# Routed experts behind attention and an MLP: two token tiles at a time, h made transposed, rows gathered an expert ahead

## The chip, the cores and the metric

The kernel runs on one core of a Trainium2 chip. The metric is the device time of one execution in microseconds (us); the median of three runs is given. A profile is one further execution, recorded by the hardware profiler.

## The reference

Three parts follow one another. Only the third is touched by most of the change.

1. Attention with a window of 128 over 4 batches, 8 heads, 576 positions, head size 64.
2. An MLP on the 2304 tokens of 512 features: `g = s * relu(x @ w_in)**2 + b`, `g @ w_out`, with 2048 hidden features.
3. Routed experts. A token is worked on if `x @ w_skip > 0`, else it passes unchanged. Its expert is the argmax of eight gate values:

```python
for e in range(E):                       # 8 experts, w1 512x1024, w2 1024x512
    mask = e_idx == e
    h = np.maximum(xc[mask] @ w1[e], 0.0)
    y[mask] = gate_w[mask, None] * (h @ w2[e])
out[do_compute] = xc + y
```

The reference, worked on its own drawn inputs, sends 639, 194, 63, 83, 51, 20, 167 and 143 tokens to the experts: 5, 2, 1, 1, 1, 1, 2 and 2 tiles of 128, 15 in all.

## The kernel before, in words

**Number format.** All big products use fp32r operands. Each fp32 operand is taken apart in a high part (a ScalarE cast) and a low part (VectorE, operand less high part), and a product is three matmuls: high x high, high x low, low x high.

**MLP.** `body` runs six blocks of 384 tokens; in a block, 16 slices of the hidden features (loop over `m`), each with 12 matmuls of 384 columns (`g1`) and 9 of 512 (`g2`). After a block its tokens are routed (`route`): logits, argmax, place in the list of the expert; three indirect DMAs on GpSimd (L625) write the list entries of the block, token number and gate weight, to DRAM (`lst`). In the last block the queue of SyncE (SP) also brings the first expert weights: `pump` (L637) issues a load of 512 KB for every free raw buffer, `split` (L644) makes the high and low part of one piece and frees its buffer. There are 8 pieces an expert: 0 to 3 are w1, 4 to 7 are w2. Five raw buffers (`ring`) serve the last block, one piece per `m`, and so all 16 pieces of experts 0 and 1; seven more (`more`) are added behind it. The parts of an expert lie in `eh` and `el` in one of two sets by the expert's parity.

**Routed experts.** `moe2` (L756) is a generator: `body` resumes it at certain points, so that the first tile of expert 0, made up of tokens of the first five blocks, is already worked on while the last block is routed. Entries of the last block that belong to tiles 1 and 2 of expert 0 are found by matmuls (`new`, L612), and their rows are gathered without waiting for the list in DRAM.

A tile goes through these steps. Its 128 rows come by an indirect DMA on GpSimd (`gather`, L780). TensorE turns them in four transposes (`x_t`, L786), ScalarE and VectorE make `xth` and `xtl`. `gemm1` (L795) has the tile's x as the loaded operand and w1 as the moving one: 24 matmuls of 512 columns, whose result, tokens by hidden features, ScalarE passes through relu (L799). `h_t` (L819) turns it in eight transposes into two banks; ScalarE and VectorE make `hth` and `htl` (L822, L823). `gemm2` (L805) is 24 matmuls of 512 columns. `fin` (L810) multiplies by the gate weight and adds the row, and an indirect DMA writes the rows out (L813).

**Order.** One `step` (L834) works on three tiles at once: it gathers tile n+1, does `gemm1` of tile n, then `gemm2` of tile n-1 with the turn of tile n+1's x between its halves, and last `h_t` of tile n. Rows and list entries are shifted from buffer to buffer by VectorE copies at the start of a step (`shift`, L826 and L827), ahead of the gather. ScalarE, VectorE and GpSimd take the order of the program here (`manual_schedule`). The splits of a step stand between its other work; `ahead` limits them to 4 pieces past the expert in work, 12 from its start.

**Branches.** The number of tiles of an expert is known only on the chip. `chain` (L882) has a branch per tile, up to `KMAX`, then a loop; `leave` (L871) is the step that goes over to the next expert. A `hint` after `gemm1` tells TensorE's instruction fetch which way the next branch goes.

Of the kernel before, what the change touches and what calls it, by code (L numbers as in the profile page):

```python
# [21 lines left out]
TB = 384  # L22
# [4 lines left out]
KMAX = (6,) + (2,) * 7  # L27
AHEAD = (0, 0, 1, 1, 1, 0, 0, 0)
BIG = 1 << 20
LE = 128 * 32  # L30
RING, MORE = 5, 7
UB = 3
CONV = (6, 7, 8, 9, 10, 11, 12)


def body(tc, q_in, k_in, vl, wm, we, wg, wgt, s_in, b_in, mask_in, cst_in, rout_in, ids_in, out):
# [488 lines left out]
    def route(j):  # L525
# [111 lines left out]
    def pump(eng=nc.sync):  # L637
        while ws.free and ws.loaded < 8 * NE:
            t, i = divmod(ws.loaded, 8)
# [4 lines left out]
    def split(t, i):  # L644
        n = 8 * t + i
# [38 lines left out]
    for j in range(NB):  # L684
# [15 lines left out]
        for m in range(NM):  # L700
# [26 lines left out]
            if j == NB - 1:  # L727
                split(*divmod(m, 8))
# [9 lines left out]
class Stream:  # L738


    def __init__(self):
        self.loaded, self.split, self.places, self.free, self.at = 0, 0, RING, [], {}

    def state(self):
        return self.loaded, self.split, self.places, list(self.free), dict(self.at)

    def back_to(self, st):
        self.loaded, self.split, self.places, self.free, self.at = *st[:3], list(st[3]), dict(st[4])
# [7 lines left out]
def moe2(tc, L):  # L756
# [4 lines left out]
    xg = [C.tile([128, DM], F32, name=f"xg{i}") for i in range(3)]  # L761
    lt = [C.tile([128, 2], U32, name=f"lt{i}") for i in range(3)]
    ls = [C.tile([128, 2], U32, name=f"ls{i}") for i in range(4)]
    la = C.tile([128, NE, NTILE, 2], U32, name="la")
    og = C.tile([128, DM], F32, name="og")
    xth = C.tile([128, DM], F32R, name="xth")
    xtl = C.tile([128, DM], F32R, name="xtl")
# [4 lines left out]
    extra = []  # L772
    bank = lambda tag, name, bufs=1: psum.tile([128, 512], F32, name=name, tag=tag, bufs=bufs)

    def gather(e, k, rows=NT, a=0):
        listed = e or not isinstance(k, int) or k not in (1, 2)
        if listed:
            nc.vector.tensor_copy(lt[a], la[:, e, k, :])
        idx = la[:, e, k, 0:1] if isinstance(k, int) and listed else lt[a][:, 0:1]
        nc.gpsimd.indirect_dma_start(  # L780
            out=xg[a], out_offset=None, in_=x2d[0:rows], in_offset=bass.IndirectOffsetOnAxis(ap=idx, axis=0),
            bounds_check=rows - 1, oob_is_err=False)

    def x_t(a=0):
        for k in range(4):
            last = nc.tensor.transpose(p_x[:, k * 128:(k + 1) * 128], xg[a][:, k * 128:(k + 1) * 128], ident)  # L786
        nc.scalar.copy(xth, p_x)
        nc.vector.tensor_tensor(out=xtl, in0=p_x, in1=xth.bitcast(F32), op=ALU.subtract)
        return last

    def gemm1(p, f, ks=range(4)):
        n = 3 * ks[0]
        todo = [(k, x, w[p, k]) for k in ks for x, w in ((xth, eh), (xth, el))] + [(k, xtl, eh[p, k]) for k in ks]
        for k, x, w in todo:
            nc.tensor.matmul(p_h[f], lhsT=x[:, k * 128:(k + 1) * 128], rhs=w[:, f * 512:(f + 1) * 512],  # L795
                             start=n == 0, stop=n == 11)
# [4 lines left out]
    def gemm2(p, f, cs=None):  # L801
# [7 lines left out]
    def fin(n):  # L809
        nc.vector.scalar_tensor_tensor(out=og, in0=p_o, scalar=lt[2][:, 1:2].bitcast(F32), in1=xg[2],  # L810
                                       op0=ALU.mult, op1=ALU.add)
# [12 lines left out]

    def shift(a):
        nc.vector.tensor_copy(lt[a + 1], lt[a])  # L826
        nc.vector.tensor_copy(xg[a + 1], xg[a])  # L827

    def hint(e, k):

        if e < NE and k < NTILE:
            tc.mark_branch_hint_location(f"tile{e}_{k}", hint=K[e] > k, engines=[mybir.EngineType.PE])

    def step(at, e1, e2, ahead, n=0, wider=0, then=None):  # L834
# [3 lines left out]
        pieces = list(range(ws.split, min(ahead, 8 * NE)))  # L838
        if e2 is not None:
            shift(1)  # L840
            shift(0)
        if at is not None and at not in ((0, 1), (0, 2)):
            gather(*at)

        def more(n):
            for _ in range(min(n, len(pieces))):
                split(*divmod(pieces.pop(0), 8))
        more(2)
        if e1 is not None:
            gemm1(e1 % 2, 0)  # L850
            more(2)
            gemm1(e1 % 2, 1)
            if then:
                hint(*then)
            for _ in range(min(wider, RING + MORE - ws.places)):
# [179 lines left out]
```

## Time and profile before

| | |
|---|---|
| Runs, median (lowest to highest) | 761.05 us (760.36 to 761.53) |
| Profiled execution | 759.11 us |
| its span | 757.0 us |
| TensorE (PE) busy | 731.1 us, 97% of the span |
| VectorE (DVE) busy | 532.4 us, 70% |
| ScalarE (ACT) busy | 384.4 us, 51% |
| GpSimd (POOL) busy | 53.7 us, 7% |

The span is the time between the first and the last instruction of the profile; the execution's own time is somewhat longer. PEld is the weight load that goes before a matmul; it may overlap PE. A busy TensorE is not TensorE at its peak, since a matmul is counted from its start to its modelled end: the spacing of starts tells what one costs. The routed experts' full steps run from about 568 us to the end.

### The profile page before, as it was taken

What the parts mean: (1) busy time and instruction counts of PE and PEld (TensorE: products, weight loads), DVE (VectorE), ACT (ScalarE), POOL (GpSimd) and SP (SyncE); (2) the same over time, 40 slices, a digit from 0 to 9 for tenths busy, and PEclk for the clock granted to TensorE, in tenths of its full rate; (3) what the DMA queues carried; (4) which work ended last, traced back from release to release, by engine and by line L of the source; (5) the groups of instructions that cost most, each with busy time, mean ns of one, the idle gap of its engine ahead of it and who ended that gap; (6) DMA issues with size and microseconds to landing.
All of it is one profiled execution on the core that took longest, in us unless ns stands there. A gap on an engine that the chain in (4) does not pass through costs nothing. (4 is left out here: it accounts for less than half of the span.)

```text
span 757.0 us, 12740 instructions
## 1 busy us (share of the span) xinstructions
PE 731.1 (97%) x4328; PEld 611.4 (81%) x4328; DVE 532.4 (70%) x1618; ACT 384.4 (51%) x909; POOL 53.7 (7%) x58
## 2 busy tenths in 40 slices
PE   7889999999999999999999999999999999899996
PEld 4568888888888888888888888989887878677884
DVE  4989999666686676777676665899642343999551
ACT  6767777544454445555564332545432243777440
POOL 0000000000001000100001000100211211112111
PEclk9689999999999999999999999999999999999999
DMA  8976341522313112422222111765443451898000
GB/s 248 304 261 195 117 124 50 164 77 73 92 47 132 53 57 67 147 71 74 57 88 95 43 42 29 271 174 167 126 153 106 137 189 44 287 349 324 18 23 16
DMA packets 50591, 96.38 MB, mean 127 GB/s; under 512 B 8554, under 2 KB 25962, under 8 KB 50496
## 3 DMA queue, kind: packets, MB, share of 16 engines
q1 hardware_dynamic: 45600, 85.82, 35.8%
q0 software_dynamic: 2976, 5.59, 2.3%
q10 hardware_dynamic: 1920, 3.80, 1.7%
q8 instruction: 47, 0.77, 0.4%
q14 instruction: 48, 0.39, 0.2%
HBM read 83.83 MB, written 13.65 MB: 129 GB/s over the span
## 5 line engine op out<-in xcount | busy, mean ns | idle before, releaser
L128 PE MATMUL h_ps<-xh,wh 128*128 128x384 f32 x380 | 132.5, 349 | 0.0
L128 PE MATMUL h_ps<-xh,wl 128*128 128x384 f32 x380 | 128.8, 339 | 0.4 <-DVE wl L70 0.4
L128 PE MATMUL h_ps<-xl,wh 128*128 128x384 f32 x380 | 128.6, 338 | 0.0
L460 ACT ACTIVATE r<-h_ps 128x384 f32<-128x384 f32 x96 | 47.1, 490 | 132.0 <-PE h_ps L128 111.9
L461 DVE SCALAR_TENSOR_TENSOR r<-r,sb 128x384 f32<-128x384 f32 x96 | 59.2, 616 | 64.0 <-ACT r L460 59.2
L522 DVE CUSTOM_DVE_ANT_0 junk<-x,hp 128x512 bf16<-128x512 f32 x135 | 92.8, 687 | 1.6
L171 ACT ACTIVATE tp<-tp,stat 128x256 f32<-128x256 f32 (+2 forms) x160 | 74.8, 469 | 28.0 <-DVE stat L163 27.9
L128 PE MATMUL acc<-wh,gh 128*128 128x512 f32 x288 | 86.8, 409 | 0.5 <-ACT gh L470 0.5
L128 PE MATMUL acc<-wh,gl 128*128 128x512 f32 x288 | 83.0, 397 | 0.0
L128 PE MATMUL acc<-wl,gh 128*128 128x512 f32 x288 | 82.4, 394 | 0.0
L471 DVE SCALAR_TENSOR_TENSOR gl<-r,sb,gh 128x384 fp32r<-128x384 f32 x96 | 59.0, 615 | 29.6 <-ACT gh L470 28.0
L470 ACT ACTIVATE gh<-r,sb 128x384 fp32r<-128x384 f32 x96 | 59.2, 616 | 40.5 <-DVE r L461 38.2
L128 PEld LDWEIGHTS h_ps<-xh,wh 128*128 128x128 f32 x380 | 71.8, 189 | 4.7 <-issue 1.4
L128 PEld LDWEIGHTS h_ps<-xl,wh 128*128 128x128 f32 x380 | 71.9, 189 | 2.4
L128 PEld LDWEIGHTS h_ps<-xh,wl 128*128 128x128 f32 x380 | 71.8, 189 | 0.7 <-DVE wl L70 0.7
L128 PEld LDWEIGHTS acc<-wh,gl 128*128 128x128 f32 x288 | 54.1, 189 | 13.2 <-DVE gl L471 0.4
L128 PEld LDWEIGHTS acc<-wl,gh 128*128 128x128 f32 x288 | 54.1, 188 | 12.6
L163 DVE CUSTOM_DVE_ANT_0 tp<-s_ps,masks 128x256 f32<-128x256 f32 (+2 forms) x160 | 52.9, 377 | 9.2 <-PE t_ps L126 4.0
L128 PEld LDWEIGHTS acc<-wh,gh 128*128 128x128 f32 x288 | 49.8, 188 | 7.9 <-issue 1.4
L625 POOL DMA_INDIRECT lst<-pay,di x18 | 18.8, 1047 | 470.7 <-DVE di L623 466.8
L805 PE MATMUL p_o<-wh,hth 128*128 128x512 f32 x120 | 48.9, 407 | 0.4 <-ACT hth L822 0.4
L795 PE MATMUL p_h<-wh,xth 128*128 128x512 f32 x120 | 48.8, 407 | 0.5 <-ACT hth L822 0.4
(138 smaller groups left out, 1245.0 us busy)
## 6 DMA issues: line engine op xcount, KB each, us to landing
ring<-we SPq DMA_DIRECT2D x36, 512.0 KB
w_words<-wm SPq DMA_DIRECT2D x30, 512.0 KB
hp<-wgt SPq DMA_DIRECT2D x45, 256.0 KB
more<-we SPq DMA_DIRECT2D x21, 512.0 KB
vt<-vl SPq DMA_DIRECT2D x32, 192.0 KB
x2d<-x SPq DMA_DIRECT2D x17, 256.0 KB
out<-x SPq DMA_DIRECT2D x17, 256.0 KB
more<-we ACTq DMA_DIRECT2D x7, 512.0 KB
```

The lines of the kernel that those rows point to most:

```text
L128: i = f(*args, **kw)
L163: anchor['v'] = nc.vector.tensor_tensor_reduce(out=t[0:nr, i, c0:c0 + n], in0=ps[i][0:nr, c0:c0 + n], in1=masks[0:nr, 2 * units[u][1] + i, ...
L171: anchor['s'] = nc.scalar.activation(out=t[0:nr, i, c0:c0 + n], in_=t[0:nr, i, c0:c0 + n], func=ACTF.Exp, scale=-1.0, bias=st[0:nr, 0, i:i ...
L460: nc.scalar.activation(out=r, in_=hp, func=ACTF.Relu)
L461: nc.vector.scalar_tensor_tensor(out=r, in0=r, scalar=sb[:, 0:1], in1=r, op0=ALU.mult, op1=ALU.mult)
L470: nc.scalar.activation(out=gh, in_=r, func=ACTF.Identity, bias=sb[:, 1:2])
L471: i = nc.vector.scalar_tensor_tensor(out=gl, in0=r, scalar=sb[:, 1:2], in1=gh.bitcast(F32), op0=ALU.add, op1=ALU.subtract)
L522: nc.vector.tensor_tensor_reduce(out=junk, in0=x2t[j, t], in1=w, scale=1.0, scalar=0.0, op0=ALU.mult, op1=ALU.add, accum_out=lgs[j][:, t, ...
L625: i = nc.gpsimd.indirect_dma_start(out=lst, out_offset=bass.IndirectOffsetOnAxis(ap=di[:, t:t + 1], axis=0), in_=pay[:, t, :], in_offset=N ...
L795: nc.tensor.matmul(p_h[f], lhsT=x[:, k * 128:(k + 1) * 128], rhs=w[:, f * 512:(f + 1) * 512], start=n == 0, stop=n == 11)
L805: last = nc.tensor.matmul(p_o, lhsT=h[:, c * 128:(c + 1) * 128], rhs=ww[:, o:o + 512], start=c == 0 and i == 0, stop=c == 7 and i == 2)
```

## The change

- Two tiles of an expert are worked on together (`pair`). In `wide` w1 is the loaded operand and x of both tiles, 256 columns, the moving one. The result is h already transposed (hidden features by tokens), in four banks of two slices each; ScalarE writes `relu` as the high part and VectorE takes the low part straight from the bank. `h_t` is left only for a tile that goes alone (`single`, and tile 0 of expert 0).
- The rows of both first tiles of expert e+1 are gathered at the start of expert e, whether it has a second tile or not, into buffers that take turns (`one`, three of them, `two`, two of them). The shifts are gone; list entries are read in place in `la`. A pair leaves its second tile's w2 work to the next expert and copies its rows and entry to a buffer of `one`.
- Pieces are split in another order (`NEED`): behind an expert's w1 work the w1 pieces of the expert two further on, and w2 pieces in their own expert.
- The ring in the last MLP block has two raw buffers in place of five, the later seven stay.
- The three list writes of the last block go behind the gather of tile 2 (`issue_after(go)`), and the second `new` matmuls go ahead of most of tile 0's `gemm2`.
- Branches: expert 0 has `tile0_3` and in it `tile0_5`; every other expert one on a second tile and in it one on a third, with a loop by pairs (left out below). The hints stand at other places.

Core of the diff (where a "..." stands, removed functions, which are shown above, and small edits are left out):

```diff
-KMAX = (6,) + (2,) * 7
-AHEAD = (0, 0, 1, 1, 1, 0, 0, 0)
...
-RING, MORE = 5, 7
+RING, MORE = 2, 7
...
+LAST = NE - 1
+LATE = 2
...
+W1, W2 = range(4), range(4, 8)
+NEED = [[(2, i) for i in W1], [(3, i) for i in W1]]
+NEED += [[(e, i) for i in W2] + [(e + 2, i) for i in W1 if e + 2 < NE] for e in range(2, NE)]
+PIECES = [(e, i) for e in range(2) for i in range(8)] + [p for ps in NEED for p in ps]
...
         for t in range(TPB):
-            i = nc.gpsimd.indirect_dma_start(
-                out=lst, out_offset=bass.IndirectOffsetOnAxis(ap=di[:, t:t + 1], axis=0),
-                in_=pay[:, t, :], in_offset=None, bounds_check=NE * LE - 1, oob_is_err=False)
+            with tc.issue_after(go) if j == NB - 1 else ExitStack():
+                i = nc.gpsimd.indirect_dma_start(
+                    out=lst, out_offset=bass.IndirectOffsetOnAxis(ap=di[:, t:t + 1], axis=0),
+                    in_=pay[:, t, :], in_offset=None, bounds_check=NE * LE - 1, oob_is_err=False)
...
+        while ws.free and ws.loaded < len(PIECES):
             ws.at[ws.loaded] = ws.free.pop(0)
-            eng.dma_start(out=ws.at[ws.loaded], in_=we[t, i])
+            eng.dma_start(out=ws.at[ws.loaded], in_=we[PIECES[ws.loaded]])
...
+    def split():
+        n = ws.split
+        t, i = PIECES[n]
...
-    xg = [C.tile([128, DM], F32, name=f"xg{i}") for i in range(3)]
-    lt = [C.tile([128, 2], U32, name=f"lt{i}") for i in range(3)]
...
+    rows = lambda name, pool=C: pool.tile([128, DM], F32, name=name)
+    one, two = [rows("one0"), rows("one1"), None], [None, rows("two1")]
+    la = C.tile([128, NE, NTILE + 1, 2], U32, name="la")
+    og = rows("og")
+    xth = C.tile([128, 4, 256], F32R, name="xth")
+    xtl = C.tile([128, 4, 256], F32R, name="xtl")
     r = C.tile([128, FE], F32, name="r2")
-    hth = C.tile([128, FE], F32R, name="hth")
-    htl = C.tile([128, FE], F32R, name="htl")
+    hth = C.tile([128, 8, 256], F32R, name="hth")
+    htl = C.tile([128, 8, 256], F32R, name="htl")
...
+    def gather(e, k, to, n=NT):
+        return nc.gpsimd.indirect_dma_start(
+            out=to, out_offset=None, in_=x2d[0:n],
+            in_offset=bass.IndirectOffsetOnAxis(ap=la[:, e, k, 0:1], axis=0), bounds_check=n - 1, oob_is_err=False)
+    def x_t(x, s):
         for k in range(4):
-            last = nc.tensor.transpose(p_x[:, k * 128:(k + 1) * 128], xg[a][:, k * 128:(k + 1) * 128], ident)
-        nc.scalar.copy(xth, p_x)
-        nc.vector.tensor_tensor(out=xtl, in0=p_x, in1=xth.bitcast(F32), op=ALU.subtract)
+            last = nc.tensor.transpose(p_x[:, k * 128:(k + 1) * 128], x[:, k * 128:(k + 1) * 128], ident)
+        to, px = slice(s * 128, s * 128 + 128), p_x.rearrange("p (k n) -> p k n", k=4)
+        nc.scalar.copy(xth[:, :, to], px)
+        nc.vector.tensor_tensor(out=xtl[:, :, to], in0=px, in1=xth[:, :, to].bitcast(F32), op=ALU.subtract)
         return last
...
+    def wide(p, then=None):
+        for b, ps in enumerate((*p_h, *p_t)):
+            for c in (2 * b, 2 * b + 1):
+                cs, n = slice(c * 128, c * 128 + 128), 0
+                todo = [(k, x, w[p, k]) for k in W1 for x, w in ((xth, eh), (xth, el))] + [(k, xtl, eh[p, k]) for k in W1]
+                for k, x, w in todo:
+                    nc.tensor.matmul(ps[:, c % 2 * 256:c % 2 * 256 + 256], lhsT=w[:, cs], rhs=x[:, k, :],
+                                     start=n == 0, stop=n == 11)
+                    n += 1
+            if b == 1 and then:
+                hint(*then)
+            h, l, ps = hth[:, 2 * b:2 * b + 2, :], htl[:, 2 * b:2 * b + 2, :], ps.rearrange("p (c n) -> p c n", c=2)
+            nc.scalar.activation(out=h, in_=ps, func=ACTF.Relu)
+            nc.vector.scalar_tensor_tensor(out=l, in0=ps, scalar=0.0, in1=h.bitcast(F32), op0=ALU.max, op1=ALU.subtract)
+    def gemm2(p, s, f, cs=None):
         for c in cs or range(4 * f, 4 * f + 4):
             w, o = 4 + c // 2, (c % 2) * 512
             for i, (h, ww) in enumerate(((hth, eh[p, w]), (hth, el[p, w]), (htl, eh[p, w]))):
-                last = nc.tensor.matmul(p_o, lhsT=h[:, c * 128:(c + 1) * 128], rhs=ww[:, o:o + 512],
+                last = nc.tensor.matmul(p_o, lhsT=h[:, c, s * 128:s * 128 + 128], rhs=ww[:, o:o + 512],
                                         start=c == 0 and i == 0, stop=c == 7 and i == 2)
         return last
...
+    def fin(x, e, k):
+        nc.vector.scalar_tensor_tensor(out=og, in0=p_o, scalar=la[:, e, k, 1:2].bitcast(F32), in1=x,
                                        op0=ALU.mult, op1=ALU.add)
-        nc.vector.tensor_copy(ls[n], lt[2])
         nc.gpsimd.indirect_dma_start(
-            out=out, out_offset=bass.IndirectOffsetOnAxis(ap=ls[n][:, 0:1], axis=0), in_=og, in_offset=None,
+            out=out, out_offset=bass.IndirectOffsetOnAxis(ap=la[:, e, k, 0:1], axis=0), in_=og, in_offset=None,
             bounds_check=NT - 1, oob_is_err=False)
...
-            fs = slice(f * 512, (f + 1) * 512)
-            nc.scalar.copy(hth[:, fs], p_t[f])
-            nc.vector.tensor_tensor(out=htl[:, fs], in0=p_t[f], in1=hth[:, fs].bitcast(F32), op=ALU.subtract)
...
+            fs, pt = slice(f * 4, f * 4 + 4), p_t[f].rearrange("p (c n) -> p c n", c=4)
+            nc.scalar.copy(hth[:, fs, 128:], pt)
+            nc.vector.tensor_tensor(out=htl[:, fs, 128:], in0=pt, in1=hth[:, fs, 128:].bitcast(F32), op=ALU.subtract)
...
+    def conv(pieces, n=8):
+        for p in pieces[:n]:
+            assert PIECES[ws.split] == p
+            split()
+        del pieces[:n]
...
+    def rest(e):
+        return (one[0], 0, 2) if e == 0 else (one[e % 3], e, 0)
+    def next_rows(e):
+        if e < LAST:
+            gather(e + 1, 0, one[(e + 1) % 3])
+            gather(e + 1, 1, two[(e + 1) % 2])
+    def single(e):
+        todo = list(NEED[e])
+        own = [p for p in todo if p[0] == e]
+        new = [p for p in todo if p[0] != e]
+        conv(own, 2)
+        gemm1(e % 2, 0)
+        conv(own)
+        gemm1(e % 2, 1)
+        if e != LATE:
+            hint(e + 1, 1)
+        conv(new, 2)
+        gemm2((e - 1) % 2, 1, 0)
+        if e < LAST:
+            x_t(one[(e + 1) % 3], 0)
+        conv(new)
+        gemm2((e - 1) % 2, 1, 1, (4, 5))
+        if e == LATE:
+            hint(e + 1, 1)
+        gemm2((e - 1) % 2, 1, 1, (6, 7))
+        fin(*rest(e - 1))
+        h_t()
+    def last_two(e, rows0, rows1):
+        new = [p for p in NEED[e] if p[0] != e]
+        conv(new, 2)
+        gemm2(e % 2, 0, 0)
+        if e < LAST:
+            x_t(one[(e + 1) % 3], 0)
+        conv(new)
+        hint(e + 1, 1)
+        gemm2(e % 2, 0, 1)
+        fin(*rows0)
+        to = rest(e)
+        nc.vector.tensor_copy(to[0], rows1[0])
+        nc.vector.tensor_copy(la[:, e, to[2], :], la[:, e, rows1[2], :])
+    def pair(e, rows0, rows1, k):
+        left = rest(e if e == 0 else e - 1)
+        own = [p for p in NEED[e] if p[0] == e] if e else []
+        conv(own, 1)
+        gemm2((e - (e > 0)) % 2, 1, 0)
+        x_t(rows1[0], 1)
+        conv(own)
+        gemm2((e - (e > 0)) % 2, 1, 1)
+        fin(*left)
+        wide(e % 2, (e, k))
         st = ws.state()
         with tc.If(K[e] > k, preferred_fallthrough_block=True, label=f"tile{e}_{k}") as c:
-            step((e, k), e, prev2, 8 * e + 12, k % 2, 2 if e == 0 else 0, (e, k + 1))
-            chain(e, k + 1, e)
+            with tc.For_i(k, K[e], 2) as kk:
...
+            last_two(e, rows0, rows1)
         ws.back_to(st)
         with c.Else():
-            leave(e, prev2)
...
+    def expert(e):
+        next_rows(e)
+        st = ws.state()
+        with tc.If(K[e] > 1, preferred_fallthrough_block=True, label=f"tile{e}_1") as c:
+            pair(e, (one[e % 3], e, 0), (two[e % 2], e, 1), 2)
+        ws.back_to(st)
+        with c.Else():
+            single(e)
...
-        gemm2(0, 0)
+        go = gemm2(0, 1, 0, (0, 1))
+        gemm2(0, 1, 0, (2, 3))
...
+    for k in (1, 2):
...
+        last_gather = gather(0, k, one[k % 2])
         if k == 1:
-            with tc.issue_after(mark):
-                last = gemm2(0, 1, (4,))
-            mark, new = yield last.ins
+            mark, new = yield go.ins
     with tc.issue_after(mark):
-        last = gemm2(0, 1, (5, 6))
+        last = gemm2(0, 1, 1, (4, 5, 6))
     with tc.issue_after(last.ins):
-        last = x_t(1)
+        last = x_t(one[1], 0)
     with tc.issue_after(last.ins):
-        gemm2(0, 1, (7,))
-    yield
-    fin(1)
+        last = gemm2(0, 1, 1, (7,))
+    with tc.issue_after(last.ins):
+        x_t(one[0], 1)
+    yield last_gather.ins
+    fin(two[1], 0, 0)
...
+        one[2], two[0] = rows("one2", E), rows("two0", E)
+        for x in (one[2], two[0]):
+            nc.gpsimd.memset(x, 0.0)
+        more = [E.tile([128, 1024], F32, name=f"more{i}") for i in range(MORE)]
...
+        nc.scalar.dma_start(out=la[:, 1:NE], in_=lv[:, 1:NE, 0:NTILE + 1])
...
         with hand:
...
+            gather(0, 3, one[2])
+            gather(0, 4, two[0])
+            wide(0)
+            ws.free.extend(more)
+            L.pump(nc.scalar)
+            gemm2(0, 0, 0)
+            x_t(one[2], 0)
+            hint(0, 3)
+            gemm2(0, 0, 1)
+            fin(one[1], 0, 1)
+            gather(1, 0, one[1])
+            gather(1, 1, two[1])
+            st = ws.state()
+            with tc.If(K[0] > 3, preferred_fallthrough_block=True, label="tile0_3") as c:
+                pair(0, (one[2], 0, 3), (two[0], 0, 4), 5)
+            ws.back_to(st)
+            with c.Else():
+                x_t(one[1], 0)
+                conv(list(NEED[0]))
+            for e in range(1, NE):
+                expert(e)
+            gemm2(LAST % 2, 1, 0)
+            gemm2(LAST % 2, 1, 1)
+            fin(*rest(LAST))
```

## Rows read from the trace of the kernel before

**Rows 1.** Windows: us busy of PE, PEld, DVE, ACT, POOL; clock, DMA share, GB/s.

```profile
643.00:656.00 13.00, 11.17 (x55) 8.94 (x54) 12.97 (x21) 9.15 (x12) 2.31 (x2) 1.00 0.73 265
...
706.00:719.00 13.00, 13.00 (x66) 10.71 (x65) 4.76 (x13) 3.32 (x6) 2.04 (x2) 1.00 0.09 25
```

**Rows 2.** Chain of waits, one step on TensorE: start us, us, what.

```profile
626.65 5.59 PE p_h L795 x24
632.24 2.80 PE p_o L805 x12
635.04 0.44 PE p_x L786 x4
...
638.28 0.87 PE p_t L819 x8
```

**Rows 3.** Waits of PE from 470 us: total us, times, longest.

```profile
PE p_x L786 <- DMA xg<-x2d,la: 4.7, 4, 1.8
```

**Rows 4.** Groups by line, PEld, 520 us on: busy us, mean ns, idle before.

```profile
L795 PEld LDWEIGHTS p_h<-wl,xth 128*128 128x128 f32 x120 | 22.6, 189 | 4.6
...
L544 PEld LDWEIGHTS l_ps<-wg_sb,hp 128*128 128x128 f32 x16 | 1.9, 191 | 0.1
```

**Rows 5.** Chain of waits, the start of the experts' stage.

```profile
564.59 0.56 PE new L612 x6
...
566.71 0.66 PE p_x L786 x4
...
568.10 5.88 PE p_h L795 x24
```

**Rows 6.** Timeline, PE, PEld at the end: start, us; [idle before].

```profile
743.74 0.50 PE L805 MATMUL p_o<-wh,hth 128*128 128x512 f32 x1 [0.28 <-ACT hth L822]
...
744.46 0.19 PEld L805 LDWEIGHTS p_o<-wh,htl 128*128 128x128 f32 x1 [0.43 <-DVE htl L823]
...
749.46 0.40 PE L805 MATMUL p_o<-wh,htl 128*128 128x512 f32 x1
```

**Rows 7.** Timeline of PE in an MLP block: starts of g2 and g1 matmuls.

```profile
504.29 0.86 PE L128 MATMUL acc<-wh,gh 128*128 128x512 f32 x3
...
506.39 0.34 PE L128 MATMUL h_ps<-xh,wh 128*128 128x384 f32 x1
...
508.47 0.86 PE L128 MATMUL acc<-wh,gh 128*128 128x512 f32 x3
```

**Rows 8.** Chain of waits, the logits' matmuls.

```profile
552.90 2.58 PE l_ps L544 x24
```

**Rows 9.** Timeline of DVE in a step with eight splits.

```profile
643.02 0.17 DVE L826 COPY lt<-lt 128x2 uint32<-128x2 uint32 x1 [2.32 <-issue]
...
643.97 1.22 DVE L70 TENSOR_TENSOR wl<-ring,wh 128x1024 fp32r<-128x1024 f32 x1
...
654.38 1.28 DVE L823 TENSOR_TENSOR htl<-p_t,hth 128x512 fp32r<-128x512 f32 x2
655.58 0.16 DVE L826 COPY lt<-lt 128x2 uint32<-128x2 uint32 x1
```

**Rows 10.** Timeline of POOL and ACT where the experts' stage starts.

```profile
563.27 1.01 POOL L780 DMA_INDIRECT xg<-x2d,lt  x1 [21.13 <-DVE di L621]
...
568.49 1.05 POOL L780 DMA_INDIRECT xg<-x2d,lt  x1 [0.30 <-issue]
...
567.46 0.59 ACT L787 CAST xth<-p_x 128x512 fp32r<-128x512 f32 x1 [7.11 <-PE p_x L786]
...
572.91 0.60 ACT L799 ACTIVATE r<-p_h 128x512 f32<-128x512 f32 x1 [4.87 <-PE p_h L795]
```

**Rows 11.** Timeline, last MLP block: SP's issues of raw loads, one cast.

```profile
521.82 13.08 SPq L641 DMA_DIRECT2D ring<-we  x4
...
527.62 1.05 ACT L651 CAST wh<-ring 128x1024 fp32r<-128x1024 f32 x1 [0.36 <-PE acc L128]
```

**Rows 12.** Windows view, the stretch of 1 us behind that load.

```profile
525.00:526.00 1.00, 1.00 (x7) 0.87 (x6) 1.00 (x2) 0.00 (x0) 0.00 (x0) 1.00 0.03 8
```

More of the change, by code (lines that the diff above doesn't have):

```diff
@@ L727, in body @@
             if j == NB - 1:
-                split(*divmod(m, 8))
+                split()
     last = g2(NB - 1, NM - 1)
@@ L794, in gemm1 @@
         for k, x, w in todo:
-            nc.tensor.matmul(p_h[f], lhsT=x[:, k * 128:(k + 1) * 128], rhs=w[:, f * 512:(f + 1) * 512],
-                             start=n == 0, stop=n == 11)
+            nc.tensor.matmul(p_h[f], lhsT=x[:, k, 0:128], rhs=w[:, f * 512:(f + 1) * 512], start=n == 0, stop=n == 11)
             n += 1
@@ L829, in hint @@
     def hint(e, k):
-        if e < NE and k < NTILE:
+        if e < NE:
             tc.mark_branch_hint_location(f"tile{e}_{k}", hint=K[e] > k, engines=[mybir.EngineType.PE])
[L834 to L855, printed above, removed]
-                ws.free.append(extra[ws.places - RING])
-                ws.places += 1
-        if at is not None and e1 is not None and e2 is None:
-            x_t()
-        more(8)
-        if e2 is not None:
-            gemm2(e2 % 2, 0)
-            if at is not None:
-                x_t()
-            gemm2(e2 % 2, 1)
-            fin(n)
-        if e1 is not None:
-            h_t()
-            L.pump(nc.scalar)
@@ L871, in leave @@
-    def leave(e, prev2):
-        if e + 1 < NE:
-            step((e + 1, 0), e, prev2, 8 * e + 12, 2 + e % 2, MORE, (e + 1, 1))
-        else:
-            step(None, e, prev2, 8 * NE, 2)
-            shift(1)
-            gemm2(e % 2, 0)
-            gemm2(e % 2, 1)
-            fin(3)
-    def chain(e, k, prev2):
-        if k == KMAX[e]:
-            st = ws.state()
-            with tc.If(K[e] > k, preferred_fallthrough_block=True, label=f"tile{e}_{k}") as c:
-                for kk in range(k, k + AHEAD[e]):
-                    step((e, kk), e, e, 0, kk % 2)
-                with tc.For_i(k + AHEAD[e], K[e], 1) as kk:
-                    step((e, bass.ds(kk, 1)), e, e, 0)
-                leave(e, e)
-            ws.back_to(st)
-            with c.Else():
-                leave(e, e)
-            return
+    def conv(pieces, n=8):
+        for p in pieces[:n]:
+            assert PIECES[ws.split] == p
+            split()
+        del pieces[:n]
@@ L896, in chain @@
         st = ws.state()
         with tc.If(K[e] > k, preferred_fallthrough_block=True, label=f"tile{e}_{k}") as c:
-            step((e, k), e, prev2, 8 * e + 12, k % 2, 2 if e == 0 else 0, (e, k + 1))
-            chain(e, k + 1, e)
+            with tc.For_i(k, K[e], 2) as kk:
+                for n, rw in enumerate((rows0, rows1)):
+                    gemm2(e % 2, n, 0)
+                    gemm2(e % 2, n, 1)
+                    fin(*rw)
+                for n, rw in enumerate((rows0, rows1)):
+                    nc.vector.tensor_copy(la[:, e, rw[2], :], la[:, e, bass.ds(kk + n, 1), :])
+                    gather(e, rw[2], rw[0])
+                for n, rw in enumerate((rows0, rows1)):
+                    x_t(rw[0], n)
+                wide(e % 2)
@@ L900, in chain @@
+            last_two(e, rows0, rows1)
         ws.back_to(st)
         with c.Else():
-            leave(e, prev2)
-    for x in xg[::-1]:
+            last_two(e, rows0, rows1)
+    def expert(e):
[6 more added lines that the diff above has]
+            single(e)
+    for x in (one[1], one[0], two[1]):
@@ L909, in moe2 @@
     nc.sync.dma_start(out=la[:, 0, 0:3], in_=lv[:, 0, 0:3])
-    gather(0, 0, NT - TB, 2)
+    gather(0, 0, two[1], NT - TB)
     yield
     p_x = bank("at", "p_x")
-    x_t(2)
+    x_t(two[1], 0)
     with tc.issue_after((yield)):
@@ L964, in moe2 @@
         with hand:
-            for e in range(NE):
-                chain(e, 1 if e else 2, e - 1 if e else None)
+            gather(0, 3, one[2])
[22 more added lines that the diff above has]
+            fin(*rest(LAST))
     yield
```

44 lines of the change are left out of this document (7 added, 37 removed).

## Prediction

> **What bounds the kernel now.** I first read the page's busy shares (TensorE 97%), then the routed experts' stage in the windows view, because the diff acts after 560 us almost alone. In the stretches of about one tile TensorE is busy throughout at granted clock 1.00 (2.4 GHz) while VectorE has 4.8 us of work in 13; only among the experts of one tile does TensorE fall to 11.2 of 13 while VectorE is busy for 12.97 [rows 1]. The chain of waits gives a tile's price on TensorE: 5.59 us for w1's 24 matmuls, twice 2.80 for w2's 24, 0.44 for the turn of x, 0.87 for the eight turns of h, 12.49 together [rows 2]. The waits view names the one repeated stall: four waits for gathered rows, 4.7 us in all [rows 3]; all four lie before one-tile experts, where the gather is issued behind VectorE's copies. So the stage is bound by TensorE's instruction stream, with VectorE close behind in four slots.
>
> **The stage, by parts.** 120 weight loads of one kind at 8 per tile are 15 tiles [rows 4], which agrees with the tiles per expert (5, 2, 1, 1, 1, 1, 2, 2). Experts 0, 1, 6 and 7 form five full pairs (0's first tile is done ahead, alone), experts 2 to 5 go singly, and no pair has an empty half. From the first w1 matmul of tile 1 (568.10) to the end of the last w2 matmul (749.46 and 0.23) TensorE takes 181.6 us [rows 5, 6]. Its work there is 14 x (5.59 + 5.59 + 0.87) + 13 x 0.44 = 174.4 us; 7.2 us are waits and restarts.
>
> **Turns of h.** Ten tiles in pairs need none: 10 x 0.87 = -8.7 us. They go off the path entirely, as TensorE ran them between matmuls. At the end the last turn also left a wait of 0.28, and a weight load behind it waited 0.43 for the second part of h [rows 6]: half a us more, gone because the last expert is a pair.
>
> **Two tiles at a time.** Each pair replaces 48 w1 matmuls of 512 columns by 96 of 256, so weight loads double: 480 small matmuls in place of 240. No fp32r matmul of 256 columns is in the trace. Nine of 512 start in 2.10 us (233 ns each) and twelve of 384 in 2.08 us (173) [rows 7]. The straight line gives 113 at 256, plain proportion 115 to 116; I take 115 as nearest to the 384 row. Below, the load itself is the floor: 24 matmuls of 9 columns, each with a load, take 2.58 us, 107.5 each [rows 8], and their load rows last as long (191 against 189 ns) as those of fp32r [rows 4]. Above, I add the 512 row's excess over its columns (233 - 213 at 2.4 GHz) to that floor: 127. So the ten tiles cost 480 x 0.115 = 55.2 us (51.6 to 61.0) against 10 x 5.59 = 55.9.
>
> A row shows how far a load hides: twelve matmuls of 384 columns with as many loads take 173 ns each, less than the 107.5 of a load and the 160 of the columns one after the other [rows 7, 8]. The Trainium skill (TensorE: Matmul & The Clock Gate, "The mechanism" of Part 3) says that a weight load overlaps a running matmul only where the two use different row groups; here both use all 128 rows. By that rule each added load would stand bare; the trace disagrees at 384 columns, and 256 is not shown.
>
> **Relu and split out of PSUM.** The four banks end about 2.8 us apart. Each needs a ScalarE and a VectorE pass, about 0.60 us by the relu of before [rows 10] and 0.64 by the split of h (1.28 for two [rows 9]); the second multiplication reads the banks in the order in which they end. Cover: 4.2 us of w2 matmuls before the last bank's h is read. Without it a pair would wait about 1.2 us.
>
> **Rows an expert ahead, no shifts.** The gathers no longer stand behind VectorE's copies, but are issued about 12 us before use. The 4.7 us of waits go [rows 3]. What is late next is VectorE. In a one-tile slot of before it went from one shift to the next in 12.56 us without a break (643.02 to 655.58), 0.95 of it copies that the change drops (643.02 to 643.97) [rows 9]; TensorE's slot is 12.49. Without the copies VectorE needs 11.6, and TensorE paces the slots. The bound is a branch that costs VectorE as it did once, 2.32 us of issue [rows 9]: 11.6 + 2.3 - 12.5 = 1.4 per slot, 5.7 for four. I take 0.
>
> **From single to pair.** A pair begins with w2 of the tile that is left, so after expert 5 the turn of h is followed by its reader at once. At 743 this cost about 0.5 us with VectorE idle [rows 6]; now up to two splits can stand ahead on VectorE, each over 1 us as the casts that run beside them [rows 11]. Between 0.5 and 2.8 I take 1.5, the middle.
>
> **The start.** The pair of tiles 1 and 2 needs both gathers before its first matmul, tile 2's gather until now stood behind the three list writes on GpSimd (gathers at 563.27 and 568.49 [rows 10]). The change puts these writes behind it and moves the second "new" matmuls, which ended at 565.15, ahead of most of w2's [rows 5], so the gather can start at 564.6 and its rows land 3.4 us later, as the first did (563.27 to the turn at 566.71), at 568.0. Turn 0.66, conversion 0.59: the first wide matmul at about 569.35, 1.25 later than 568.10. Bounds: 0.6 if the conversion alone shows, 3 if one list write stays ahead on POOL. ScalarE's list load waits for the later list writes and delays the first relu, at 572.91 before [rows 10], to about 574.3; the four banks are free then, and TensorE reads h only at 580.4. The gathers of tiles 3 and 4 land near 581, needed at 583.
>
> **Raw buffers, 5 to 2, in the last block.** A load issued at 521.82 has left the DMA by 525 (8 GB/s in the us after that [rows 12]); with two buffers it is needed by the next cast but one, at 527.62 [rows 11]. The margin is 2.6 us, so 0; if a load were late, the cast would stop ScalarE's queue, with the relu and g of the block behind it, and TensorE. SP's queue still takes loads, router weights and x rows in turn. In the experts' stage nine buffers replace twelve; a one-tile slot asks for eight loads, 4.2 MB in 12.5 us, 336 GB/s; the bound is that the DMA carries less, as in the first such slot (265 GB/s at share 0.73, [rows 1]), but nine buffers filled beforehand leave only 23 of the 32 loads to those slots.
>
> **Small edits.** Each pair copies its second tile's rows and list entry into the buffer of the tile that is left (VectorE, about half a us, as much as one shift of before): hidden in 23 us of TensorE work. The second gather of a one-tile expert brings nothing and costs GpSimd 1.0 us [rows 10] of a queue that is mostly idle; two more memsets there stand ahead of the gathers of tiles 3 and 4. Seven raw loads are issued at once behind the first relus instead of two at a time; their first use is 30 us later. I cost all at nothing; were the copies bare on the path they would add 2.5 us.
>
> **Sum.** TensorE's list is 55.2 + 4 x 5.59 + 4 x 0.87 + 14 x 5.59 + 12 x 0.44 = 164.7 us. Start 569.35, list 164.7, single to pair 1.5, and 1.0 for restarts (before had about 1.4 that no wait names): end at 736.55 against 749.7, 13.1 less. The last result's way out after it (7.3 us) stays. The profiled execution took 759.11 (span 757.0), so 746.0; the median of the timed runs, 761.05, is 1.94 above it, so **748 us**. Its own range: with loads at 107.5 ns 744; with the small terms at their bad ends 751.
>
> **Rivals.**
> - VectorE paces the one-tile slots, at 2.3 us per branch: 748 + 5.7 = 754. For it: VectorE was busy without a break there [rows 1]; against: the gap came once in four slots.
> - Wide matmuls at 127 ns: 748 + 480 x 0.012 = 754. For it: nothing in the trace runs load and columns so evenly matched; against: the line through 384 and 512.
> - Gathers are late anyway, as loads crowd the DMA in the one-tile slots: 748 + 4.7 = 753. Then the change does not do what it says. Against: they have a whole slot.
> - **Slower: TensorE's jumps.** The hint on a branch now stands 2.3 to 5.6 us of matmuls ahead of nine of the twelve branches, where before a whole second multiplication and the turns (6.9 us) lay between. Eight branches go to their Else (0's last, the second of experts 1, 6 and 7, four singles), and four blocks end in a jump over one. If each of the twelve costs what VectorE's branch cost, 2.3 us [rows 9], that is 27.6: 776. It turns the result slower from 13.1/12 = 1.1 us each. Against: TensorE showed no wait at any branch.
> - Raw loads that land more than 5.8 us after issue stop each of 14 splits; at 1 us each 762.
> - Loads that stand bare in the wide matmuls: 480 x 107.5 ns = 52 us more, 800. This is the rule named above; the 384 row speaks against it.
>
> **How the numbers follow.** Forecast 55%, VectorE 15%, slow small matmuls 13%, late gathers 5%, jumps 6%, raw loads 4%, bare loads 2%. The range 741 to 759 reaches from the load floor without the restarts (748 - 3.6 - 2.5, and one more us for a quicker start) to two of the middling rivals together (748 + 5.7 + 5.5); it leaves out the last three and some of each tail. A difference of 0.2% (1.5 us) is what a measurement can tell. Faster holds the first four cases, 88%, less 6% for several terms going bad at once: 0.82; same 0.05; slower 0.13.
>
> **What would show it.** In the profile after: 96 wide matmuls of a pair from start to end in 11.0 us (over 12.2 is the second rival); no wait of TensorE for gathered rows; slots of 12.5 us for experts 2 to 5, with VectorE showing gaps; the first wide matmul between 569 and 570; no ScalarE wait for a raw load before 550; no hole in TensorE at a branch. The prediction is wrong if TensorE's holes after 569 add up to over 5 us, or if a wide matmul starts more than 120 ns after the one before.

## The result: slower by 1%, and what the profile after shows

The changed kernel took 768.23 us (764.8 to 771.46, 6 runs) beside 760.44 us for the kernel before (6 runs): ratio 1.010, 95% interval 1.0069 to 1.013. A second set gave 768.38 us and 1.013 (1.0107 to 1.0153). Forecast were 748 us and a range of 741 to 759: wrong in sign, and the time lies outside the range. The profiled execution took 771.46 us, its span is 769.7; it is the slowest of the six, 3.2 us above their median.

What the change was made of came out as forecast. Two rows of the TensorE timeline give the wide matmuls of the first pair, its start and the first matmul behind it (start us, us, instruction, idle before it):

```profile
571.55 0.39 PE L811 MATMUL p_h<-xth,wh 128*128 128x256 f32 x1 [0.68 <-ACT xth L791]
...
582.86 0.40 PE L824 MATMUL p_o<-wh,hth 128*128 128x512 f32 x1
```

96 matmuls in 11.31 us are 117.8 ns each. Over all 480 wide matmuls the starts lie 116.7 ns apart on average, the few steps of over 200 ns left out. What was lost stands in the waits of TensorE, total us, times, longest:

```profile
PE p_x L789 <- DMA one<-x2d,la: 12.3, 3, 10.4
PE p_o L824 <- DVE og L829: 6.0, 5, 2.0
```

Before, rows cost 4.7 us in four waits [rows 3], 4.1 of it in the experts' stage; now one wait alone costs 10.4, and the second group is new. Here is the long wait, traced back. Timelines of VectorE, GpSimd and TensorE; the bracket is the idle time before the instruction and what ended it:

```profile
641.10 1.05 POOL L831 DMA_INDIRECT out<-og,la  x1 [17.30 <-DVE og L829]
...
648.21 0.17 DVE L900 COPY la<-la 128x2 uint32<-128x2 uint32 x1 [6.93 <-DMA out<-og,la]
...
658.81 0.75 DVE L829 SCALAR_TENSOR_TENSOR og<-p_o,la,one 128x512 f32<-128x512 f32 x1
...
659.84 1.03 POOL L831 DMA_INDIRECT out<-og,la  x1 [14.66 <-DVE og L829]
...
661.48 6.98 POOL L783 DMA_INDIRECT one<-x2d,la  x1 [0.61 <-issue]
...
665.21 2.35 DVE L77 TENSOR_TENSOR wl<-more,wh 128x1024 fp32r<-128x1024 f32 x2
...
673.88 1.12 PE L789 MATMUL p_x<-cst,one 128*128 128x128 f32 x4 [10.39 <-DMA one<-x2d,la]
```

The copy of the list entry, one of the pair's small copies, overwrites `la[:, e, 0]`. The write-out of that tile's rows reads its offsets there, so the copy waits until the write-out has left, 7 us after its issue. VectorE runs in order, so the splits, the low part of x and the `fin` in expert 2's slot queue behind it. That `fin`'s write-out stands ahead of the next gather on GpSimd, so that gather starts only at 661.48, just when the splits that had been held free raw buffers and their loads fill the DMA. Windows of 5 us (busy us of PE, PEld, DVE, ACT, POOL; granted clock; DMA share; GB/s):

```profile
645.00:650.00 5.00, 4.10 (x20) 3.08 (x19) 1.05 (x2) 3.07 (x5) 0.17 (x1) 1.00 0.22 77
...
655.00:660.00 5.00, 3.80 (x17) 2.78 (x16) 5.00 (x6) 2.51 (x4) 0.16 (x1) 1.00 0.94 323
660.00:665.00 5.00, 3.48 (x15) 2.45 (x14) 5.00 (x6) 3.18 (x4) 4.39 (x2) 1.00 1.01 403
665.00:670.00 5.00, 0.00 (x0) 0.00 (x0) 2.56 (x3) 0.00 (x0) 4.45 (x2) 0.58 1.01 405
670.00:675.00 5.00, 1.12 (x5) 1.13 (x6) 0.00 (x0) 0.00 (x0) 0.00 (x0) 0.50 0.63 244
675.00:680.00 5.00, 5.00 (x15) 3.86 (x15) 3.15 (x4) 2.48 (x3) 0.00 (x0) 0.56 0.20 60
```

Read VectorE's 1.05 of 5 us at 645 first: it stands while the DMA falls to 0.22, for no buffer comes free. Then the DMA is full until 670, GpSimd takes 6.98 us to issue one gather (1.0 before [rows 10]), and TensorE has nothing. The long issue goes with VectorE more closely than with the DMA: VectorE runs six splits without a break from 660.67 to 667.56, and the gather ends 0.90 us behind the last of them. Of the 10.4 us, by estimate, some 5.7 lie in the issue itself (6.98 us in place of the 1.3 that the same gather took in another kernel below). In the hole its granted clock falls from 1.00 to 0.50 (1.2 of 2.4 GHz), and the first 11 matmuls behind it start 0.43 us apart in place of 0.233 [rows 7]: about 2.2 us more.

The waits of `p_o` are five. A pair does w2 of its first tile last and leaves w2 of its second to whatever comes next; where that is another pair, or the end, the two w2 products follow each other at once and both write the single bank `acc1`. TensorE has to wait there until VectorE has read it; which of the five waits are the bank's, the second experiment shows:

```profile
589.90 0.50 PE L824 MATMUL p_o<-wh,hth 128*128 128x512 f32 x1 [0.84 <-DVE og L829]
...
615.45 0.47 PE L824 MATMUL p_o<-wh,hth 128*128 128x512 f32 x1 [2.02 <-DVE og L829]
...
708.07 0.47 PE L824 MATMUL p_o<-wh,hth 128*128 128x512 f32 x1 [1.16 <-DVE og L829]
...
732.56 0.47 PE L824 MATMUL p_o<-wh,hth 128*128 128x512 f32 x1 [0.94 <-DVE og L829]
...
756.62 0.47 PE L824 MATMUL p_o<-wh,hth 128*128 128x512 f32 x1 [1.00 <-DVE og L829]
```

The one at 708.07 is the step from the last one-tile expert to a pair, for which the prediction had a term of 1.5 us.

### The profile page after: what moved, and what is told of

Read it like the earlier page. It is cut to its first block, busy times and chain, and to the rows that moved or that the text cites. A ratio compares the mean times of both kernels' runs of the same rounds, so it can differ in the third digit from the quotient of the medians.

```text
span 769.7 us, 12920 instructions
## 1 busy us (share of the span) xinstructions
PE 727.2 (94%) x4488; PEld 616.6 (80%) x4488; DVE 522.3 (68%) x1544; ACT 373.9 (49%) x889; POOL 65.1 (8%) x64
## 4 chain that ended last, share of the span: by engine, by line
PE 51%; issue 27%; DMA 14%; DVE 4%; POOL 1%; SPq 1%; POOLq 0%; another core or an unknown queue 0%; ACT 0%
PE h_ps L135 19%; PE acc L135 19%; DMA out<-og,la 11%; PE o_ps L135 4%; PE s_ps L135 4%; PE t_ps L135 3%; PE p_h L799 1%; DMA w_words<-wm 1%; DVE tp L170 1%; PE t_ps L133 1%; DVE hp L404 1%; PE s_ps L133 1%; DVE hp L406 1%; POOL two L783 1%; DMA k<-k_in 0%
## 5 line engine op out<-in xcount | busy, mean ns | idle before, releaser
L824 PE MATMUL p_o<-wh,htl 128*128 128x512 f32 x120 | 48.3, 402 | 0.1
```

Of the source, the lines that this page charges most:

```text
L824: last = nc.tensor.matmul(p_o, lhsT=h[:, c, s * 128:s * 128 + 128], rhs=ww[:, o:o + 512], start=c == 0 and i == 0, stop=c == 7 and i == 2)
```

## The experiments

Theory A: the copy of the list entry holds VectorE, hence late rows and the long hole. Theory B: the raw loads fill the DMA, and rows come late whatever is done about the copy. Theory C: the single result bank costs the 6 us of `p_o`. Theory J: TensorE's jumps, that is, branches whose code has to be fetched first. Each kernel was timed in five rounds beside the kernel before. The first four shared a chip (before: 759.03 us), as did the next four (759.96) and the last two (759.5).

**The changed kernel once more.**

> The changed kernel once more, beside the others. In its first profile TensorE waited 12.3 us for gathered rows (10.4 of it in one hole among the one-tile experts), 6.0 us for the result bank, and ran some 5 us at the lower clock after the hole. Theory A (the copy of a list entry waits for the write-out that reads the entry, holds VectorE 7 us, and everything behind it comes late) and theory B (rows come late because the raw loads fill the DMA, whatever VectorE does) both expect the hole again at the same expert, 8 to 12 us, time 765 to 771. If the hole is an accident of one execution, it is missing here and the time is below 760.

768.38 us. Waits for rows 10.5, longest 10.1; the gather again takes 6.98 us; `p_o` 6.0. The hole belongs to the kernel, not to one execution.

**The copy taken away from its reader.** The entry goes to a slot of `la` that no write-out reads:

```diff
-        return (one[0], 0, 2) if e == 0 else (one[e % 3], e, 0)
+        return (one[0], 0, 2) if e == 0 else (one[e % 3], e, NTILE)
...
         fin(*rest(e - 1))
+        nc.vector.tensor_copy(la[:, e, NTILE, :], la[:, e, 0, :])
```

> The second tile's list entry is copied to a free column of the list buffer, so the copy has nothing to wait for; a one-tile expert makes the same copy of its own entry. Theory A: the waits of VectorE for the write-out (12.2 us in three) go, the result of expert 1's last tile is written 6 to 7 us sooner, the gather behind it on GpSimd starts 6 to 7 us sooner, the 10.4 us hole shrinks to under 3, no clock loss there; 755 to 759 against 768. Theory B: VectorE's waits go but rows still land when the raw loads are through, hole 7 us or more, 765 to 768.

759.33 us, ratio 1.0002 (0.9988 to 1.0016): 9.0 us less than the changed kernel beside it. Waits of TensorE, then the gather that had taken 6.98 us:

```profile
PE p_o L824 <- DVE og L829: 4.8, 4, 2.0
PE p_x L789 <- DMA one<-x2d,la: 3.6, 2, 2.2
```

```profile
657.04 1.98 POOL L783 DMA_INDIRECT one<-x2d,la  x1 [0.61 <-DVE htl L841]
```

Theory A holds for the long hole: the time is 0.3 us above its range and far from theory B's. The 3.6 us that stay are about what stood in this stage before, 4.1.

**Two result banks.** The first tile's product goes to `acc2`, free by then:

```diff
-                last = nc.tensor.matmul(p_o, lhsT=...
+                last = nc.tensor.matmul(p_o[s], lhsT=...
```

> The w2 product of the second tile (or the left one) goes to another PSUM bank than that of the first; nothing else. Theory C (one result bank, read by VectorE between two w2 products that now follow each other at once, stops TensorE five times): the 6.0 us of waits for the bank go; if they are on the path, 4 to 6 us less than the changed kernel, 762 to 764. Theory B's and A's hole stays. Rival: the time saved is spent waiting for rows instead, since these land by the DMA's clock: hole grows, 767 to 768.

763.39 us, ratio 1.0054 (1.0036 to 1.0071): 5.0 less. `p_o` waits 3.1 us in place of 6.0: the waits at 589.90 and 615.45 are gone, the other three stay. At 708 the edit leaves both products in one bank (`s` is 1 for both). At 732 and 757 the two products are in two banks now and TensorE waits as before, so those 1.9 us are not the bank's. Rows still wait 8.2 us, with the gather at 6.99. So theory C holds for 2.9 us. The other 2.1 lie elsewhere: rows wait 2.3 us less in this profile, and 2.0 us are lost ahead of expert 3.

**Both.**

> Both edits. Theories A and C together: 12 of the hole and its clock loss and 5 of the bank, 749 to 753, which would be faster than the kernel before (760.4) by some 1%. Theory B and C: 762 to 764. If the sum of the two single edits is not reached, the stalls share their time.

756.0 us, ratio 0.9953 (0.9934 to 0.9971): 12.4 less than the changed kernel, and 3.3 less than with the entry alone, about the 2.9 of the two bank waits. It is faster than the kernel before, but 8 us from the prediction's time and 3 above the range expected here; the two single gains, 9.0 and 5.0, do not add up in full. Two holes are left. First, rows still come late; the waits of TensorE:

```profile
PE p_x L789 <- DMA one<-x2d,la: 4.3, 3, 2.2
PE p_h L799 <- DVE wl L77: 3.6, 1, 3.6
```

Second, the stop ahead of expert 3's first matmul. The waits view calls it a wait for a split; the load that goes before the same matmul says that it waited for nothing that the profile shows:

```profile
652.66 0.19 PEld L799 LDWEIGHTS p_h<-wh,xth 128*128 128x128 f32 x1 [3.81 <-issue]
652.69 0.47 PE L799 MATMUL p_h<-wh,xth 128*128 128x512 f32 x1 [3.60 <-DVE wl L77]
```

That place is an Else, and its hint is the only one among the one-tile experts that stands 6 matmuls and 8 turns ahead of the branch rather than behind the first multiplication.

**The late hint early.**

```diff
-        if e != LATE:
-            hint(e + 1, 1)
+        hint(e + 1, 1)
...
-        if e == LATE:
-            hint(e + 1, 1)
```

> Entry elsewhere and two banks, and expert 2 too gives the hint on its successor's branch behind its first multiplication, as the others do, not 6 matmuls and 8 turns ahead of the branch. Jump theory: the one hole of 3.6 us before expert 3's first matmul (its load row says issue) is TensorE's instruction fetch begun too late; it goes, waits for gathered rows stay at some 4 us: 752.5. Split theory: the wait is for VectorE's split, as the waits view names it; it stays: 756.

754.61 us, ratio 0.9925 (0.9899 to 0.9951; the interval overlaps that of the kernel with both edits, so the gain in time is not clear of noise). The hole is gone with the hint alone moved, so it was not the split. Rows now wait 5.4 us in four places, so part of the 3.6 us went there:

```profile
PE p_x L789 <- DMA one<-x2d,la: 5.4, 4, 1.7
```

**All four hints late.** The same lines, but the late place for every one-tile expert.

> Entry elsewhere and two banks, and all four one-tile experts give the hint on the next branch late, 6 matmuls and 8 turns ahead of it, as expert 2 does. Jump theory with a fixed price: three more holes of 3.6 us, 767. Jump theory with a price that depends on how full the DMA is: 0 to 2 us each, 756 to 761. Split theory: no change, 756.

758.17 us, 3.6 more than with early hints beside it. The loads ahead of the first matmuls of experts 3, 4 and 5:

```profile
650.34 0.19 PEld L799 LDWEIGHTS p_h<-wh,xth 128*128 128x128 f32 x1 [1.30 <-issue]
663.42 0.19 PEld L799 LDWEIGHTS p_h<-wh,xth 128*128 128x128 f32 x1 [0.56 <-issue]
679.07 0.28 PEld L799 LDWEIGHTS p_h<-wh,xth 128*128 128x128 f32 x1 [3.12 <-issue]
```

A jump hinted late has no fixed price: 0.6 to 3.1 us of the load's idle time here, 3.8 in the kernel with both edits, where the DMA share was 1.01 in the 5 us before the stop. The changed kernel, with the same late hint, shows only 0.61 at this place, where the share was 0.27; behind the early hints of one-tile experts it is 0.12 at most. The Trainium skill (Runtime: NRT & Kernel Launch, "Instruction fetch mechanics") says that a taken branch to a page outside the engine's window has to fetch that page by DMA before it can go on. The holes fit it. The page of every profile here has queues of kind "instruction" (0.82 MB in 50 packets in the changed kernel), and the traces keep the time of every packet, though no view prints it. At ten of the eleven late-hinted stops in these profiles, 0.5 to 3.8 us long, the first load starts 1.5 to 1.6 us after a packet of that queue has ended. In the changed kernel, with the DMA idle, the packet begins 0.2 us after the place of the hint; in six of the other eight, at a DMA share of 0.86 to 1.03, it begins 1.9 to 3.4 us after it. So the price goes mostly with how long the packet waits on a full DMA.

**Rows two experts ahead.** Four and three row buffers; for the room, six raw buffers of the later kind in place of seven.

```diff
-        if e < LAST:
-            gather(e + 1, 0, one[(e + 1) % 3])
-            gather(e + 1, 1, two[(e + 1) % 2])
+        if e + 2 < NE:
+            gather(e + 2, 0, one[(e + 2) % 4])
+            gather(e + 2, 1, two[(e + 2) % 3])
```

> Entry elsewhere and two banks, and rows gathered two experts ahead (4 and 3 row buffers in place of 3 and 2; 6 raw buffers in place of 7, for the room). Theory that the gathers still compete with the raw loads of their own slot: the waits for gathered rows (4.3 us, 3 places) go to under 0.5, the hole before expert 3 stays at 3.6: 752. Rival: the waits move to VectorE's splits or to the raw loads, as the slot is bound by the DMA there (share 0.94 to 0.98 from 635 to 650): 755 to 757.

754.38 us, ratio 0.9926 (0.99 to 0.9952; the interval overlaps that of its control below, so it is the waits that decide here). No wait for rows is left in the experts' stage; the hole before expert 3 stays at 3.0:

```profile
PE p_h L799 <- ACT wh L659: 3.0, 1, 3.0
```

**Its control: six raw buffers, nothing else.**

> Entry elsewhere and two banks with 6 raw buffers more in place of 7 and nothing else, the control for the rows two ahead. If the rows' lead did it there: waits for rows stay at 3 to 5 us, 756. If the smaller number of raw loads in flight did it: they fall below 1.5, 753 to 754.

755.62 us, ratio 0.9954 (0.9935 to 0.9972), as with seven; rows wait 4.1 us. Their waits went by the gathers' lead, then, not by the smaller number of loads.

**The changed kernel with three later raw buffers in place of seven.** `RING, MORE = 2, 3`.

> The changed kernel with 3 raw buffers more in the experts' stage in place of 7 (5 in all). Theory that the raw loads in flight hold up the gathers: the gather that took 6.98 us on GpSimd takes under 2, and the longest wait for rows falls from 10.4 to 5 or less; raw loads come later and cost some of it back: 762 to 765. Theory that the copy of the list entry alone decides: the wait stays 8 or more: 768 or more.

765.12 us, ratio 1.0065 (1.0043 to 1.0088). Rows wait 2.1 us, the longest 1.7, and that gather takes 1.31 us, though the copy is still held, for 4.59 us:

```profile
646.29 0.17 DVE L900 COPY la<-la 128x2 uint32<-128x2 uint32 x1 [4.59 <-DMA out<-og,la]
...
660.69 1.31 POOL L783 DMA_INDIRECT one<-x2d,la  x1 [0.60 <-issue]
```

So the held copy alone does not make the 10 us hole; it also takes many raw buffers. Fewer buffers do two things at once, fewer loads on the DMA and no long run of splits on VectorE (two here, then a gap of 1.77 us), and this run does not tell them apart. The traces speak for the splits: the long gathers of all three profiles end 0.9 us behind the last split of a run of six, and the kernel with all four edits, with the DMA as full, issues one in 1.31 us. Splits run there too; why a gather gets in between those and not between these is open. What fits theory B are the waits of some 4 us that stay when the copy is cured. The kernel stays slow since TensorE still waits 6.4 us for `p_o` and stops for 4.8 before expert 3. That stop is not the jump's: ScalarE had waited for raw loads (12.1 us in seven waits), and TensorE goes on when ScalarE's cast of a piece ends.

**All four edits.**

> All four edits: entry elsewhere, two banks, rows two experts ahead (6 raw buffers more in place of 7), expert 2's hint early. If the jump and the late rows are separate losses, both go: no wait for rows over 0.5 us, no hole over 1 us before expert 3, 4 us under either alone: 751. Rival, that the slots of experts 2 to 5 are bound by the DMA once nothing else stops them: waits for splits or raw loads come in their place, 754 as with either alone.

749.72 us (747.27 to 750.54), ratio 0.9874 (0.9852 to 0.9896): faster than either kernel by more than 1%. Windows:

```profile
640.00:645.00 5.00, 5.00 (x25) 4.09 (x24) 4.88 (x5) 3.95 (x6) 2.55 (x2) 1.00 0.97 343
645.00:650.00 5.00, 5.00 (x28) 4.15 (x27) 4.74 (x7) 4.27 (x6) 0.25 (x1) 1.00 1.04 402
650.00:655.00 5.00, 5.00 (x23) 4.04 (x22) 5.00 (x6) 4.42 (x7) 4.02 (x3) 1.00 1.03 383
655.00:660.00 5.00, 5.00 (x25) 3.99 (x25) 4.31 (x5) 4.11 (x5) 0.01 (x1) 1.00 0.99 385
```

TensorE is busy throughout with the DMA full all the while: here a full DMA costs nothing, and the rows that are gathered in it are needed only two experts later. A gather in this stretch:

```profile
651.45 1.31 POOL L783 DMA_INDIRECT one<-x2d,la  x1 [0.67 <-DVE htl L841]
```

What remains of waits from the first wide matmul on:

```profile
687.13 0.48 PE L824 MATMUL p_o<-wh,hth 128*128 128x512 f32 x1 [1.15 <-DVE la L882]
...
712.06 0.50 PE L824 MATMUL p_o<-wh,htl 128*128 128x512 f32 x1 [0.84 <-DVE one L897]
...
735.71 0.47 PE L824 MATMUL p_o<-wh,hth 128*128 128x512 f32 x1 [1.00 <-DVE og L829]
...
741.15 0.40 PE L824 MATMUL p_o<-wh,htl 128*128 128x512 f32 x1
```

From 571.62, its first wide matmul, to 741.38 are 169.8 us; the prediction had 167.2.

## Why the prediction was wrong

The sum said 746.0 for a profiled execution, and it was 771.46: 25.5 us more, and the median of the runs lies 20 above the forecast. By steps:

- **Small edits: the step that failed.** "Each pair copies its second tile's rows and list entry ... hidden in 23 us of TensorE work". The working costed the copies by their length and did not ask what they wait for. A copy that overwrites a list entry has to wait for the write-out that reads it: 12.2 us of VectorE in three copies, 6.9 in one. With that copy's target changed, 9.0 us went. In the profiles the waits for rows fall from 12.3 to 3.6 us, and with the hole go some 2.2 us at half clock behind it and a wait of 1.2 for VectorE's half of x at 656.68.
- **A wait that no step named.** Two w2 products that follow each other on one bank: 4.8 us of waits were booked there, of which 2.9 went with a second bank. The other 1.9, at 732 and 757, stay with two banks, so they are something else. In the kernel with all four edits the first of them stands at the product's third matmul (712.06), which starts when VectorE's copy of the rows has ended; why it waits for that stays open. The part on relu asked whether the banks of h come free and did not ask it of the result bank.
- **Rows an expert ahead, no shifts.** "The 4.7 us of waits go": wrong by itself too. Not all of the 4.7 lay before one-tile experts, as the prediction read it: 0.6 stood in the last MLP block (544.63), and 1.2 before expert 6 (689.57), which has two tiles. With A and C mended 4.3 us stay; the lead of one expert does not do while the slot's raw loads fill the DMA, a lead of two does. The rival "gathers are late anyway" had this size and 5%.
- **TensorE's jumps.** The rival of the other sign, put at twelve jumps of 2.3 us. The late hint ahead of expert 3 cost 3.8 us where the DMA was full, and 0.6 in the changed kernel (0.4 by the matmul behind it). So the mechanism exists, but it is not what made this change slower.
- **Turns of h, two tiles at a time.** Right. 116.7 ns for 115 is 0.8 us over 480. The trace shows that a load hides here: a load of 107.5 ns [rows 8] and 256 columns together take 116.7. The Trainium skill (TensorE: Matmul & The Clock Gate, "The mechanism" of Part 3) has both answers: it says that a load overlaps a running matmul only where the row group differs, which is the rule that the prediction took as a rival, and also that a load which targets "the background weight buffer" is pulled ahead. The trace disagrees with the first and fits the second.
- **VectorE next.** It did not pace the slots where it ran unheld: in the kernel with all four edits TensorE is busy 5.00 of 5 us with VectorE at 4.3 to 5.0, and its slots of one-tile experts are 12.5 us long (first loads at 648.19, 660.71 and 673.22), as forecast.
- **From single to pair.** 1.5 forecast; 1.16 at 708.07, and 1.15 at 687.13 in the last kernel. Right in size, and two splits did stand ahead on VectorE. What ended the wait is another thing than the prediction names, though: not the parts of h, of which ScalarE's were done by 707.62, but VectorE's read of the result bank, which ended at 707.91; VectorE's part of h came behind it and held the third load by 0.24.
- **The start.** 569.35 forecast, 571.55 measured. In other kernels here it was 568.56 to 571.97, with no edit near it. In five executions, this one among them, the granted clock is 0.66 to 0.70 in the window 555 to 560, ahead of it; in the other six and in the kernel before it is 1.00 there. Counted from the end of the logits' matmuls, the first wide matmul comes 15.9 to 16.0 us later in the five and 14.4 in the six: 1.6 us, which the sum could not know. What decides it stays open.
- **Raw buffers, 5 to 2.** Right: ScalarE shows no wait for a raw load in the last block.

Added up: start 2.2, rows 12.3, `p_o` 6.0, half clock 2.2, waits of 0.4 and 1.2 at 653 and 657, wide matmuls 0.8, together 25.1; less the 2.5 allowed for the step from single to pair and for restarts, 22.6. About 3 us are in no named wait. A kernel with the four edits comes within 2 us of the forecast (749.72), but that does not bear the forecast out: one of the four mends a step that it held right, the rows' lead. What the working lacked was the question of what each new instruction waits for.

## What to carry to other kernels

For every copy or write that a change adds, ask which earlier reader of the target is still under way; a write-out by list held the copy over its offsets for 2.6 us in a quiet stretch and for 4.6 to 6.9 where loads ran beside it, and the engine that waits takes everything queued behind it along. Where two products that wrote in turn with other work now follow each other, count their result banks. Rows and jumps that go by the same DMA as bulk loads need their lead measured at full DMA, not by their time in a quiet stretch.

## What the runs showed of the hardware

- How long GpSimd is occupied by issuing a gather of 128 rows goes by VectorE. From 575 us on, in all twelve profiles, 97 gathers that began with no split under way on VectorE took 0.99 to 1.05 us. The 82 that began during a split took 1.06 to 6.99, and each ended 0.87 to 0.92 us after the end of a split: 79 of them after the first that ended, the three long ones (6.98, 6.98 and 6.99) after the sixth, where VectorE's run of splits stopped. The DMA share does not decide: at 1.03 a gather took 1.31. No run changed this alone, and why the three missed five ends of splits is open.
- In the hole of 10 us the granted clock fell to 0.50, and the window 675 to 680, in which TensorE was busy throughout, still shows 0.56.
- TensorE's first load behind a late-hinted jump was idle for 0.5 to 3.8 us and started 1.5 to 1.6 us after the end of a 16 KB packet of an "instruction" queue. Behind the early hint of a one-tile expert it was idle for 0.12 us at most; behind the hint of a pair, 12 matmuls ahead, for 0.2 to 0.8.
